# Attention with sinks and expert routing in one kernel: banded heads in 64-key blocks, routing steps in other places, sink values loaded by DMA

## The chip, the cores and the metric

One core of a Trainium2 chip runs one program. The metric is the device time in microseconds (us). Five engines work side by side, each through its own list of instructions in order: PE (matrix products, with PEld for its weight loads), DVE and ACT (both read PE's accumulators, PSUM), POOL (casts, memsets, and the issue of software DMAs), and SP (issue of the other DMAs). All DMAs run on the same 16 DMA engines. Instructions wait for each other through semaphores. The order within each engine is the order of the program text: the kernel uses a manual schedule.

## The reference

There are two parts, and the second reads what the first wrote.

```
attention, B=4, H=8, S=768, D=64, scale 1/sqrt(D):
    scores = scale * q @ k^T, causal
    heads 0, 2, 6 ("retrieval"): all earlier keys
    heads 1, 3, 4, 5, 7 ("banded"): keys 0..3 (sinks) and the last 64 keys
    out = softmax(scores) @ v
x = out as 3072 tokens x 512
mixture of experts, E=8, F=1024:
    for each expert e: rows = tokens with domain_id == e
        out[rows] = relu(x[rows] @ w1[e]) @ w2[e]
```

q, k, v and the weights arrive as float32; the products are done in fp16 with float32 sums.

## The kernel before

**Attention.** Heads are taken in pairs, `PAIRS = [(0, 2), (6, 7), (1, 3), (4, 5)]`, four pairs to a batch and 16 pairs n in all (n = 4 * batch + pair). The first pair has two retrieval heads (called RR here), the second one of each kind (RS), the third and fourth two banded heads (SS). The two heads of a pair lie on the two halves of the 128 partitions, so score products contract over 64 rows and come as two row tiles.

For each pair: `load_qk` and `load_v` (SP, lines 148 and 167) bring q, k and v four pairs ahead; `cast_qk` (line 158, POOL, two pairs ahead) and `cast_v` (line 178, POOL, one pair ahead) make fp16. `cast_v` also copies the four sink rows of each banded head into the small tiles `vs` (line 182), whose other rows are zero. PE transposes q and k of the next pair (line 286) into buffers of the pool `ps_b` (two buffers of one PSUM bank); DVE copies them out (line 292) as `qT`, `kT`.

`scores` works in rounds: a round is a score tile of 1024 columns (two banks) in the pool `ps_s` (three buffers). First PE adds masks by a product with the identity (line 306, `c16s`), then the products of `kT` and `qT` (also line 306); ACT takes the exponential of the whole tile (line 343) into `eT`. RR pairs have 6 rounds, RS pairs 5, SS pairs 3. A banded head is cut in key blocks of 128, each with the 192 query columns that see it, and extra columns "s" for the sinks.

The values are multiplied in by `av_items` (line 396): `eT` is the stationary operand and v with a column of ones the moving one (65 columns), summed in a `ps_b` buffer for each head; DVE takes reciprocals (line 408) and scales into `xb` (line 409). In the loop over n, pair n's score rounds go two at a time, and between them stand the transposes of pair n + 1 and the value products of pair n - 1:

```python
        elif R == 3:
            steps = [T["q"] + A, T["k"] + B_]
        ...
        for x, step in enumerate(steps):
            if n < NPAIR:
                scores(n, range(2 * x, min(2 * x + 2, R)))
            if n >= 1 and route:
                route.pop(0)()
            run(step)
```

**Routing.** `routing_items` computes from `domain_id` where each token goes: 20 small steps, nearly all on DVE, from `one_hot` (line 466) to `rows3` (line 637). One step is taken from the list in each step of the loop, from pair 1 on. Two of the steps have products on PE (`ranks`, line 484, and `rows`, line 595), both in `ps_b` buffers.

**The seam.** The finished heads of a batch, `xb`, are stored to DRAM (`store_x`, line 420, SP). `hooks(n)`, called ahead of pair n, holds the loads, the casts, the stores (batches 0, 1, 2 at n = 5, 9, 13), and weight loads by software DMA on POOL (line 190): w1 of expert 0 at n = 6, of experts 1 and 2 at n = 12 and 13. At n = 14 POOL clears four tiles (line 825), gathers the rows of experts 0 to 3 from the first three batches by six indirect DMAs (line 663), then issues w1 of expert 3, two more gathers and w2 of expert 0 (line 197). After the last pair PE transposes the first gathered rows (`x_transpose`, line 683, DVE copies in lines 690 and 696), then does the value products of pair 15; the store of batch 3 and the gathers that need all four batches follow.

**Experts.** `layer1` (line 711 on PE, 718 on ACT) takes 256 early slots of experts 0 to 3 first, then the rest; `layer2` (lines 761, 745) and `layer2_half` (line 775) give rows that DVE copies (line 725) into `oute` tiles of the pool `opool` and POOL scatters (line 727). A fallback for uneven routing (line 932) is not taken.

The softmax here doesn't subtract the row's maximum and nothing guards it: scores larger than these inputs give would overflow.

## Time and profile before

| what | value |
|---|---|
| median of 4 runs | 214.42 us (213.64 to 216.2) |
| profiled execution | 216.23 us, span 214.5 us |
| PE busy | 188.9 us (88%) |
| PEld, DVE, ACT, POOL busy | 123.4, 96.5, 92.3, 120.5 us |
| exponentials L343, 68 of them | 57.6 us |
| score products L306 (276) and masks L306 (132) | 24.9 and 22.7 us |
| value products L396 with ve (472) | 25.5 us |
| software DMA queue q0, hardware queue q1 | 55.1% and 36.9% of 16 engines |
| HBM read and written | 56.76 and 10.49 MB |

The span runs from the first to the last instruction on the chip; the rest of the time lies around it. A row with L306 names the line of the kernel that issued it, then engine and operation, what is written and read, the count, the busy time and the mean. PE's instructions overlap, so a mean of 200 ns does not say that one starts every 200 ns. The DMA row counts how busy the 16 DMA engines were, slice by slice.

### The profile page before, as it was taken

The page shows a single profiled execution, that of the slowest core. Times are in us where ns is not written, and L with a number is a line of the kernel's source. Part 1 is how long each engine was busy: PE and PEld are TensorE (multiplying, and loading weights), DVE is VectorE, ACT ScalarE, POOL GpSimd, SP SyncE. Part 2 cuts the span into 40 slices and gives each one's busy share as a digit, 9 for nine tenths or more (in the row PEclk, how much of TensorE's full clock was granted, in tenths as well). Part 3 has the DMA queues.
Part 4 walks back from the last instruction along what each step waited for, and adds up shares of the span by engine and source line. Part 5 has one row for each costly group of instructions (what it writes and reads, how often), then busy time and mean ns, then how long its engine had stood idle before and what let it go on. Part 6 is the DMA issues. An engine that isn't in the chain of part 4 may idle for free. (4 is left out here: it accounts for less than half of the span.)

```text
span 214.5 us, 4791 instructions
## 1 busy us (share of the span) xinstructions
PE 188.9 (88%) x1959; PEld 123.4 (58%) x1959; DVE 96.5 (45%) x200; ACT 92.3 (43%) x120; POOL 120.5 (56%) x170
## 2 busy tenths in 40 slices
PE   1699888999989999969859999999999999999950
PEld 1447555666656757649748996555655565444430
DVE  1345998899887657651110212540044400333420
ACT  2567545874786688614615562005610065100000
POOL 2417765697467697277645653557847720304772
PEclk9999996999999999979988999999999999999995
DMA  6999999999999999738999999999799999961443
GB/s 199 323 289 308 287 280 310 305 343 247 284 303 343 269 207 240 170 103 223 210 239 210 213 260 219 244 187 265 150 192 220 274 212 220 286 170 50 173 152 105
DMA packets 42909, 49.79 MB, mean 232 GB/s; under 512 B 27263, under 2 KB 35712, under 8 KB 42882
## 3 DMA queue, kind: packets, MB, share of 16 engines
q0 software_dynamic: 7936, 26.75, 55.1%
q1 hardware_dynamic: 34802, 22.62, 36.9%
q8 instruction: 17, 0.28, 0.5%
q10 hardware_dynamic: 144, 0.07, 0.2%
q14 instruction: 10, 0.08, 0.1%
HBM read 56.76 MB, written 10.49 MB: 314 GB/s over the span
## 5 line engine op out<-in xcount | busy, mean ns | idle before, releaser
L343 ACT ACTIVATE eT<-sp 128x1024 f16<-128x1024 f32 (+2 forms) x68 | 57.6, 918 | 27.7 <-PE sp L306 27.7
L718 ACT ACTIVATE hT<-h 128x512 f16<-128x512 f32 (+2 forms) x48 | 32.1, 669 | 59.1 <-PE h L711 59.1
L711 PE MATMUL h<-xT,w 128*128 128x256 f16 (+2 forms) x384 | 52.9, 300 | 0.5 <-DVE xT L690 0.5
L727 POOL DMA_INDIRECT out_dram<-oute,out_i x27 | 27.1, 1002 | 38.0 <-DVE oute L725 33.5
L711 PEld LDWEIGHTS <-w 128*128 128x128 f16 x384 | 39.8, 116 | 12.1 <-DVE xT L690 0.7
L761 PE MATMUL o<-w,hT 128*128 128x512 f16 x184 | 41.9, 379 | 0.0
L725 DVE COPY oute<-o 128x512 f32<-128x512 f32 x23 | 15.9, 692 | 51.5 <-PE o L761 50.0
L663 POOL DMA_INDIRECT xe<-x_tok,map_i x24 | 24.4, 1019 | 16.4 <-issue 6.3
L761 PEld LDWEIGHTS <-hT 128*128 128x128 f16 x184 | 17.5, 98 | 19.8 <-issue 0.8
L396 PE MATMUL av<-ve,eT 128*128 128x65 f16 (+1 forms) x472 | 25.5, 200 | 1.5 <-DVE xb L409 1.1
L306 PE MATMUL sp<-qT,kT 64*128 64x192 f16 (+8 forms) x276 | 24.9, 285 | 1.8 <-DVE kT L292 1.8
L396 PEld LDWEIGHTS <-eT 128*128 128x128 f16 (+1 forms) x572 | 22.7, 104 | 6.1 <-DVE xb L409 3.0
L306 PE MATMUL sp<-c16s 128*128 128x128 f16 (+1 forms) x132 | 22.7, 283 | 1.6 <-ACT eT L343 1.4
L158 POOL CAST q<-q 128x768 f16<-128x768 f32 x15 | 12.4, 829 | 15.8 <-DMA q<-in_q_dram 11.1
L696 DVE COPY xT<-xtp 128x1024 f16<-128x1024 f16 (+1 forms) x16 | 8.8, 552 | 27.1 <-PE xtp L683 27.1
L292 DVE COPY qT<-tpq 128x768 f16<-128x768 f16 x15 | 14.3, 953 | 12.2 <-PE tpq L286 12.2
L178 POOL CAST ve<-v 128x384 f16<-128x384 f32 x32 | 16.8, 553 | 5.1 <-DMA v<-in_v_dram 4.9
L409 DVE TENSOR_TENSOR xb<-av,rcp 128x384 f16<-128x384 f32 x32 | 17.8, 557 | 1.1
L158 POOL CAST k<-k 128x768 f16<-128x768 f32 x15 | 13.4, 896 | 8.4 <-PE tpk L286 6.6
L306 PEld LDWEIGHTS <-kT 64*128 64x128 f16 (+1 forms) x276 | 11.1, 98 | 12.2 <-issue 3.9
L292 DVE COPY kT<-tpk 128x768 f16<-128x768 f16 x16 | 15.3, 954 | 3.6 <-PE tpk L286 3.5
L286 PE MATMUL tpq<-c16s,q 128*128 128x128 f16 x96 | 9.4, 242 | 5.6 <-DVE q L158 4.8
(83 smaller groups left out, 136.9 us busy)
## 6 DMA issues: line engine op xcount, KB each, us to landing
w<-in_moe_w_dram POOLq DMA_DIRECT2D x16, 1024.0 KB, 12.4
q<-in_q_dram SPq DMA_DIRECT2D x16, 384.0 KB, 6.0
k<-in_k_dram SPq DMA_DIRECT2D x16, 384.0 KB, 5.9
v<-in_v_dram SPq DMA_DIRECT2D x32, 192.0 KB, 5.6
x_tok<-xb SPq DMA_DIRECT2D x4, 768.0 KB, 6.5
out_dram<-oute,out_i POOLq DMA_INDIRECT x27, 6.7
xe<-x_tok,map_i POOLq DMA_INDIRECT x24, 7.1
c16s<-c SPq DMA_DIRECT2D x1, 336.5 KB, 5.6
```

Source lines behind the costliest of these rows:

```text
L158: eng.tensor_copy(out=t[:].rearrange("p t h d -> p h t d"), in_=q32_t[nm, n][:])
L178: nc.gpsimd.tensor_copy(out=ve_t[b][:, :, h, 0:D], in_=v_t[b, pi][:, hh])
L292: evac(out=d[:], in_=cell["ps"][:, 0:NSO].rearrange("d t p -> d p t"))
L306: nc.tensor.matmul(out=sp[rows, c : c + w], lhsT=lhsT, rhs=rhs, start=bank not in begun, stop=True, skip_group_check=True,)
L343: nc.scalar.activation(out=eT[n, r // 3][:, r % 3, c0:c1], in_=sp[:, c0:c1], func=AF.Exp, scale=scale)
L396: nc.tensor.matmul(out=ps[m0:m1, it, :], lhsT=eT[n, r // 3][:, r % 3, c : c + w], rhs=rhs, start=(x == 0), stop=(x == len(mms) - 1), skip_ ...
L409: nc.vector.tensor_tensor(out=xb[b][:, :, h * D : (h + 1) * D], in0=ps[:, :, 0:D], in1=rcp[:].unsqueeze(2).to_broadcast([P, NSO, D]), op=A ...
L663: nc.gpsimd.indirect_dma_start(out=xe_of(pr, g), out_offset=None, in_=x_d[0 : 1 + nb * S, :], in_offset=bass.IndirectOffsetOnAxis(ap=map_i ...
L711: nc.tensor.matmul(out=pv[:, a, c0:c1], lhsT=w_t[e, 1][:, c // 2, c % 2, fc * 512 + fr : (fc + 1) * 512 : 4], rhs=xT_t[e][:, c, c0:c1], st ...
L718: nc.scalar.activation(out=hT_t[e][:, 2 * f2 : 2 * f2 + 2, c0:c1], in_=pv[:, :, c0:c1], func=AF.Relu)
L727: inst = nc.gpsimd.indirect_dma_start(out=out, out_offset=bass.IndirectOffsetOnAxis(ap=out_i[:, s : s + 1], axis=0), in_=o[:], in_offset=None,
L761: nc.tensor.matmul(out=ps[:], lhsT=hT_t[e][:, f, g * P : (g + 1) * P], rhs=w_t[e, 2][:, f // 4, f % 4, :], start=(f == 0), stop=(f == 7),)
```

## The change

It has four parts.

1. **Banded heads in 64-key blocks.** The key blocks of a banded head are now 64 keys with 128 query columns each; two blocks (even and odd) stand above each other in the 128 partitions, so a band needs 768 columns. Each product is a 64x64 tile of the array (64 rows, 64 columns of weights). The sinks are 32-key products of 256 query columns, each group of queries r on partitions 32r to 32r + 31. RS pairs have 4 rounds instead of 5, SS pairs 2 instead of 3. The value products of a banded head are 6 full ones (diagonal block 0 and the sinks), 5 over the lower 64 rows and 10 over the upper 64 rows with 64 columns.
2. **Transposes.** q and k are transposed together. In pairs with two rounds they go into one `ps_s` buffer ahead of the scores, and ACT copies q; elsewhere they go to the two `ps_b` buffers after the first two rounds, and DVE copies both.
3. **Routing.** A table places each step: one_hot to place in pair 0, place2 to high in pair 1, the rest at pairs 4, 5, 8, 10, 11, 12. A step now follows the products of its loop step. `rows` sums in a `ps_s` buffer.
4. **Sinks.** The `vs` tiles hold the sinks of 15 heads (two batches), one tile for each 32-partition place, in buffers of `opool`. Three are cleared on POOL and loaded by software DMA at the start, three are cleared on DVE at n = 1 and loaded at n = 4. The 20 small copies in `cast_v` go.

```diff
-    VS = [[7, 1, 4], [3, 5]]
+    VH, VR = 15, 3
...
+    m_even = neg(np.where(up, cc < kk, cc >= kk))
+    m_odd = neg(np.where(up, cc >= kk, cc < kk))
+    m_first = neg((ii[:, :P] >= jj) & ((jj < NS) | (ii[:, :P] - jj < WIN)))
...
-        for hh, h in enumerate((hA, hB)):
-            if not retr[h]:
-                x = 1 if hh and not retr[hA] else 0
-                nc.gpsimd.tensor_copy(
-                    out=vs_t[b % 2][x][64 * x : 64 * x + NS, VS[x].index(h), :],
-                    in_=ve_t[b][0:NS, 0, h, :],
-                )
+    def vs_tile(r, bh, eng):
+        t = opool.tile([P, 1024], FP16, tag="oute", name=f"vs_{r}_{bh}")
+        eng.memset(t[:], 0.0)
+        vs_t[r, bh] = t[:, 0 : VH * (D + 1)].rearrange("p (h d) -> p h d", h=VH)
+        eng.memset(vs_t[r, bh][32 * r : 32 * r + NS, :, D : D + 1], 1.0)
+
+    def load_vs(r, bh):
+        nc.gpsimd.dma_start(
+            out=vs_t[r, bh][32 * r : 32 * r + NS, :, 0:D],
+            in_=v.rearrange("b h j d -> j (b h) d")[
+                0:NS, 2 * H * (bh + 1) - VH : 2 * H * (bh + 1), :
+            ],
+        )
...
+    def s_bin(col, hh, part):
+        res = []
+        q0, q1 = ((0, 512), (512, S))[part]
+
+        def add(k0, m, o, i0, w, kind="band"):
+            lo, hi = max(i0, q0), min(i0 + w, q1)
+            if lo < hi:
+                res.append((col + lo - q0, hi - lo, hh, k0, m, o, lo, (hh, kind)))
+
+        for o in (0, 64):
+            add(o, 64, o, 0, P)
+        for it in range(NSO):
+            k0 = it * P
+            if it:
+                add(k0, 64, 0, k0, P)
+            add(k0 + 64, 64, 64, k0 + (64 if it else P), P if it else 64)
+        if part == 1:
+            for r in range(4):
+                i0 = (P, 3 * P, 4 * P, 4 * P)[r]
+                res.append((col + 256, 256, hh, 0, 32, 32 * r, i0, (hh, "s", r)))
+        return res
...
+    def transposes(n, q_evac, wide):
+        if wide:
+            ps = ps_s.tile([P, 2, 8, P], FP16, tag="sp", name=f"tp_{n}")
+            halves = [ps[:, x] for x in range(2)]
+        else:
+            halves = [
+                ps_b.tile([P, 8, P], FP16, tag="b", name=f"tp{nm}_{n}")[:] for nm in "qk"
+            ]
...
+                nc.tensor.matmul(
+                    out=sp[o : o + m, c : c + w],
+                    lhsT=kT[n][rows, k0 : k0 + m],
+                    rhs=qT[n][rows, i0 : i0 + w],
+                    start=False,
...
+                full.append((slice(0, P), band(0), ve[:, 0, h, :], 0, 0, P))
+                for it in range(1, NSO):
+                    r = (it - 1) // 2
+                    full.append(
+                        (slice(0, P), col_of(tiles, (hh, "s", r), it * P),
+                         vs_t[r, b // 2][:, b % 2 * H + h - 1, :], it, 0, P)
+                    )
+                for it in range(1, NSO):
+                    low.append((slice(0, 64), band(it * P), ve[0:64, it, h, :], it, 0, P))
+                    for m0 in (64, 0):
+                        jt = it if m0 else it - 1
+                        upp.append(
+                            (slice(64, P), band(it * P + m0), ve[64:P, jt, h, :], it, m0, 64)
+                        )
...
+        return (fa + fb, la + lb + ua + ub) if lb else (fa, fb)
...
-            t_ = ps_b.tile([P, 512], FP32, tag="b", name="map_ps")
+            t_ = ps_s.tile([P, 1024], FP32, tag="sp", name="map_ps")
...
+        return {
+            (0, 0): (one_hot,), (0, 1): (ranks, scan), (0, 2): (own, place),
+            (1, 0): (place2, split), (1, 1): (flags, high),
+            (4, 0): (high2, high3), (4, 1): lows[0:1], (4, 2): lows[1:2], (5, 1): lows[2:3],
+            (8, 0): lows[3:4], (8, 1): lows[4:5], (8, 2): lows[5:6],
+            (10, 0): (rows,), (11, 0): (rows2,), (12, 0): (rows3,),
+        }
...
-    for i in range(2):
-        for x in range(2):
-            nc.gpsimd.memset(vs_t[i][x][:], 0.0)
+    for r in range(VR):
+        vs_tile(r, 0, nc.gpsimd)
+        load_vs(r, 0)
...
+        if n == 1:
+            for r in range(VR):
+                vs_tile(r, 1, nc.vector)
+        if n == 4:
+            for r in range(VR):
+                load_vs(r, 1)
...
+        R = len(plans[n % 4]) // 2 if n < NPAIR else 1
+        av0, av1 = av_items(n - 1) if n >= 1 else ([], [])
+        tr = []
         if n == NPAIR:
-            steps = [[lambda: x_transpose(0, 0, 1, wide=True)] + A + B_]
...
+            tr = [lambda: x_transpose(0, 0, 1, wide=True)]
+        elif n + 1 < NPAIR:
+            q_evac = nc.scalar.copy if R == 1 else nc.vector.tensor_copy
+            tr = [lambda: transposes(n + 1, q_evac, R == 1)]
+        if R == 1:
+            run(tr)
+        steps = {1: [av0 + av1], 2: [tr, av0 + av1], 3: [tr, av0, av1]}[R]
         for x, step in enumerate(steps):
             if n < NPAIR:
-                scores(n, range(2 * x, min(2 * x + 2, R)))
-            if n >= 1 and route:
-                route.pop(0)()
+                scores(n, (2 * x, 2 * x + 1))
             run(step)
+            for fn in route.get((n, x), ()):
+                fn()
```

## The prediction

> **What bounds the kernel now.** I read the page's slices first, then the table of busy time by stretch, then the timelines of DVE, POOL and PE around the seam between attention and experts; landings of single DMAs, packets and clock stretches are from the trace's own records. The weight loads in their order are called w0, w1, w2, w3 (first-layer weights of experts 0 to 3). First the DMA row of the 40 slices, then the table by stretch:
>
> ```profile
> DMA  6999999999999999738999999999799999961443
> ```
> ```profile
> 60.00:75.00 15.00, 14.55 (x244) 10.08 (x243) 11.29 (x25) 10.14 (x13) 9.57 (x20) 1.00 1.06 301
> 75.00:90.00 15.00, 14.46 (x236) 9.70 (x233) 9.71 (x19) 11.70 (x15) 9.82 (x17) 1.00 1.03 219
> 90.00:98.00 8.00, 6.07 (x77) 4.61 (x76) 3.67 (x9) 1.95 (x4) 6.18 (x7) 0.79 0.36 93
> 98.00:115.00 17.00, 13.59 (x121) 12.33 (x120) 2.07 (x3) 7.09 (x13) 9.70 (x10) 0.90 1.03 232
> ```
> The columns are stretch, length, busy time of PE, PEld, DVE, ACT and POOL, clock, DMA share, GB/s. The DMA engines are full from 2 to 90 us (slices at 9), then at 0.36 for 8 us, then full again. So attention may compute faster, but its bytes and the first three expert weights end near 91.4 whatever the engines do. What can be won is that hole: 8.0 x (1 - 0.36) = 5.1 us of DMA time.
>
> The timelines of DVE, of POOL and of PE at that seam (start, length, and in brackets the idle time before and what ended it):
>
> ```profile
> 78.49 0.56 DVE L409 TENSOR_TENSOR xb<-av,rcp 128x384 f16<-128x384 f32 x1
> ```
> ```profile
> 78.88 0.70 POOL L190 DMA_DIRECT2D w<-in_moe_w_dram  x1
> ...
> 81.11 3.63 POOL L825 MEMSET xe<- 128x1024 f16 x4
> 89.27 1.09 POOL L663 DMA_INDIRECT xe<-x_tok,map_i  x1 [4.53 <-DVE xb L409]
> ```
> ```profile
> 92.38 0.38 PE L683 MATMUL xtp<-c16s,xe 128*128 128x128 f16 x4 [1.09 <-DMA xe<-x_tok,map_i]
> 93.60 0.40 PE L683 MATMUL xtp<-c16s,xe 128*128 128x128 f16 x4 [0.84 <-DMA xe<-x_tok,map_i]
> ...
> 109.83 0.63 PE L683 MATMUL xtp<-c16s,xe 128*128 128x128 f16 x8 [3.42 <-DMA xe<-x_tok,map_i]
> ```
> Why the hole is there: the normalised heads of pair 11 are ready at 79.05, SP then stores batch 2 (issued 79.07, landed 88.4), and only then do the six first gathers leave POOL, one each 1.3 us (1.0 busy, 0.3 issue). The fourth expert's weights (w3) stand behind them on POOL, at 96.9, and land at 109.3; the gathers behind w3 land after it, at 109.7. That is PE's gap of 3.42 us before 109.83. From 118.3 PE has no gap that matters (34.5 busy of 35 us from 115 to 150). The end is thus set by when the store of batch 2 is issued, not by the end of attention: PE waits at 91.3 already.
>
> **The change, part by part.** Durations are of the profiled execution: 216.23 us, span 214.5 and 1.7 around it. It lies 1.8 above the median of 214.42; PE had a half-clock stretch at 32.7 to 36.1 in it.
>
> *Pairs of two banded heads (SS), PE.* PE's timeline in pair 11, the later of them without routing:
> ```profile
> 68.94 1.04 PE L306 MATMUL sp<-c16s 128*128 128x512 f16 x4
> 69.91 0.62 PE L306 MATMUL sp<-qT,kT 64*128 64x192 f16 x12
> 70.45 0.51 PE L286 MATMUL tpq<-c16s,q 128*128 128x128 f16 x6
> ...
> 71.21 0.34 PE L396 MATMUL av<-ve,eT 128*64 128x65 f16 x5
> 71.48 0.23 PE L306 MATMUL sp<-c16s 128*128 128x64 f16 x2
> ```
> Pair 11 takes 4.46 us. Starts in the trace: masks 216 ns apart, then 312 to the first score; transposes 56 apart; value products (AV) 29.5 apart, whether 128 or 64 columns of weights; at 71.2 and 71.5 a change between 128-column and 64-column tiles shows as 122 to 129. So a change of tile shape costs 312 - 216 = 96 ns. Before there are nine such changes in an SS pair; after, six (masks, 64x64 scores, 64x32 sinks, full AV, lower halves, upper halves, transposes).
> New SS pair: 12 transposes x 56 = 0.67; masks 2 x 216 + 2 x 108 = 0.65; 28 scores in 64x64 tiles: 768 columns to a tile, at 53 ns per 128 (the score pairs of now) 0.32 if four tiles overlap, 28 x 29 = 0.81 if weight loads pace them: 0.60, towards the second, as the 64-column AV row paces at 29 to 36. 8 sink products of 256 columns: 0.11 all at once, 0.43 by twos: 0.25. AV 12 full x 29.5 = 0.35, 30 halves x 29.5 = 0.88 (0.60 if twos overlap). Switches 6 x 96 = 0.58. Sum 3.98, ends 3.3 and 4.4, against 4.46 where no routing disturbs.
> The Trainium skill (TensorEngine Tiling (Array Packing), sections Key Properties and Restrictions) speaks against this part: a change of tiling mode drains the array, and column tiling switches fast weight load off. Row: 96 ns a drain, fewer drains than before, and PEld rows of 64*64 last 104 ns like those of 128*128 (105). By the row 3.98; by the rule taken hard, weight loads that nothing hides, 36 score products x 104 ns = 3.7 us replace 0.85 and the pair takes 6.8. I keep the row: now the 64-column products start 29 to 36 ns apart, so their loads are hidden.
>
> *Transposes* go to a score buffer in SS pairs, with the query copy on ACT: 7 x 0.80 = 5.6 us onto ACT, 7 x 0.95 = 6.7 off DVE. The stall for a ps_b buffer (0.22 in pair 11) goes. Exponentials: 56 instead of 68 per kernel. Per batch 5 x 1.02 + 0.40 (two retrieval heads, RR), 3 x 1.02 + 0.70 (mixed, RS), 4 x 1.02 (two SS) = 13.3, 53.3 instead of 57.6. With the copies ACT stays at 59: no gain, but SS needs 2.85 of 4 us, so it is not the bound there. RR 4.9 and RS 4.8 (now 4.75 and 5.06 without routing) are near ACT's 9.3 for both.
>
> *Routing from pair 0.* On DVE the steps one_hot to high, about 9.5 us, fall into pairs 0 and 1, with three new memsets of about 0.6 each (0.27 for the 256-wide one, doubled). After kT of pair 1 (near 12.4) DVE has some 14.5 us queued, so the q and k copies of pair 2, the normalising of pair 0 and the k copy of pair 3 run late, to about 28. PE also waits in pair 0 for rs before the prior product, about 1.2. Pair 2 starts near 22 (21.17 now), and pairs 2 and 3 win nothing though they shed their routing (now 5.5 and 5.0): pair 4 at about 32 (31.68 now). The product of rows moves to a score buffer: nothing.
>
> *Sinks first.* POOL runs 3 x (0.95 + 0.1 + 1.0) = 6.2 us from 0.75, to 6.9 with the ve memset. Now it idles until 6.70 for v, and the next cast waits for q until 8.84: hidden; uncovered 0.2. The 20 copies of L182 (5.4 us) go; three issues (3 us) come in pair 4, ahead of casts whose data is 5 us early. c16 shrinks by 112 KB, the sinks read 92 KB: DMA unchanged.
>
> *Sum to the store.* Pairs 4 and 5 stay on DVE (high2, high3, three lows 3.9 us, copies and normalising 6.8: 10.7); 6, 7 8.1; 8, 9 9.8; 10, 11 8.1; 1.7 for keys of pair 10 delayed, as w0 is now issued earlier; pair 12 4.9: 32 + 10.7 + 8.1 + 9.8 + 8.1 + 1.7 + 4.9 = 75.3, normalised by 76 instead of 79.05. SP can then issue at 76: its last load was issued at 73.6. The store queues behind v of pair 15 (landed 77.4) and shares with w1. From first packet to landing it took about 6.4 us beside the weights (82.0 to 88.4): lands at 83.8. By the skill (DMA: Bandwidth & Descriptors, section Queues, rings and completion order: rings take turns packet by packet) its own 3.2 us (store 1, after v's landing) would double at most to 6.4 if packets were equal; same size, so the row stands. POOL is past its memsets at 83.3 in any case. w1 and w2 cannot come earlier: they stand on POOL behind casts of q and k of pairs 14 and 15, which land at 72.5 and 76.
>
> *Sum to the end.* Gathers leave at 84 to 92; they sit behind w2 in POOL's DMA queue, so the first lands at 91.8 to 92.3, as now, but the second with it: -1.0. w3 is issued at 92.8 instead of 96.9; the hole closes; w3 lands near 102.8 and the next gathers at 103.5, before PE wants them (105.4): -3.4. The half clock at 111.2 to 114.6, which follows that gap: -1.7; a copy wait at 118.3: -0.5. PE alone: -6.6. But the late gathers of expert pair 1 land at 122.4 and PE takes them at 122.74 now: they come earlier only by the filled hole, 5.1. So -5.2: **211.0 us**. The median does not move this: DMA's floor is the same in a run without the early half clock, so against 214.42 it is 3.4 less.
>
> **Rivals.**
> *The store comes no earlier* (0.20). SS pairs 6, 7, 10, 11 at 4.8 instead of 4.03, or DVE's queue, give 76 + 3 = 79. For: DVE is 95% busy in pairs 2 and 3; the new 64x64 pace is shown by no row. Against: six switches for nine. Then 214.4, within 1.5.
> *Tiles do not overlap* (0.16, slower). Place: 64x64 scores and 64x32 sinks. Price: 3072 + 2048 columns one after another at 53 ns per 128 = 2.1 instead of 0.85: SS 5.3. It decides from 4.8 on. The store is issued at 76 + 4 x 1.27 + about 1.5 (pairs 2, 3, RS) = 82.6, 3.5 later than now; all behind it moves: 214.4 + 3.5 = 218. For: the rules above. Against: pairs of row tiles start 3 to 4 ns apart, and so do 64-column pairs of L775.
> *The gathers need not wait for w2* (0.06). Then PE transposes at 87.5 and the end moves 5 more: 206. Against: every gather issued behind a weight load lands after it (7.1 us median, 2.8 at least).
>
> **Numbers.** Forecast (0.58): 211.0, own range 208.5 to 213.5. Less than 1% from 214.42, about what a measurement tells from nothing, is 212.3 to 216.6. Faster: 0.55 of the forecast, 0.06, 0.03 of the first rival: 0.64. Slower: 0.16 and a little of the first: 0.17. Same 0.19. Range 208 to 216: the forecast's own, the first rival, and the nearer part of the slower one. That the change would not do what it says is no rival: the instruction lists of the two programs show the tiles, the moved steps and the early loads.
>
> **What the changed profile would show.** Right: DMA share near 1 from 90 to 98; first gather issued near 84; store of batch 2 near 76; SS pairs near 4.0 late, pair 4 at 32; no half clock near 111; POOL's start hidden. Wrong if: SS over 4.8, or the first gather not before 88 (no gain), or PE waits at xtp L683 after 105 as long as now.

## The result: slower by about 1%, and the profile after

| | kernel before | changed kernel |
|---|---|---|
| median, all executions | 214.35 us (63: 211.55 to 217.45) | 217.01 us (42: 213.52 to 221.66) |
| ratio, 95% interval | 1 | 1.0074 (1.0049 to 1.0099) |
| profiled execution: time, span, mean clock | 216.23, 214.5 us, 0.966 | 218.41, 216.6 us, 0.956 |
| exponentials, score products, masks | 57.6 (68), 24.9 (276), 22.7 us (132) | 50.1 (56), 21.9 (468), 17.4 us (112) |
| expert pair 0 starts layer 2 (first product o2_0_0) | 129.79 us | 130.79 us |

The ratio compares, for each kernel, only the executions within 1.5% of its fastest; between the medians of all executions it is 1.012. The forecast was 211.0 us, 1.6% faster.

The DMA row of the 40 slices, then the table by stretch (length, busy PE, PEld, DVE, ACT, POOL, clock, DMA share, GB/s), of the changed kernel:

```profile
DMA  6999999999999999859999999996799999941333
```
```profile
75.00:90.00 15.00, 10.54 (x263) 7.79 (x263) 8.08 (x18) 8.34 (x9) 10.66 (x15) 0.95 1.07 233
90.00:98.00 8.00, 5.51 (x63) 4.51 (x64) 2.10 (x5) 0.57 (x1) 6.23 (x7) 0.50 0.53 119
98.00:115.00 17.00, 16.28 (x161) 15.47 (x160) 2.99 (x6) 9.08 (x17) 7.36 (x9) 0.98 0.98 222
115.00:150.00 35.00, 31.70 (x256) 22.15 (x254) 8.85 (x18) 10.16 (x19) 20.32 (x22) 0.95 1.01 227
```
PE has less to do in 75 to 90 (10.5 us busy instead of 14.5) and works at half clock from 90 to 98. From 98 to 115 it is busy 2.7 us more than before; from 115 to 150 it is busy 2.8 us less than before. So it wins the old gap and loses another. The hole in the DMA row has only gone from a share of 0.36 to 0.53.

The timeline of POOL at the seam (start, length, and in brackets idle time before and what ended it); the weight loads in it are w2, w3, and the second-layer weights of expert 0:

```profile
79.47 0.71 POOL L193 DMA_DIRECT2D w<-in_moe_w_dram  x1
...
87.49 1.10 POOL L649 DMA_INDIRECT xe<-x_tok,map_i  x1 [2.78 <-DVE rcp L395]
...
95.15 0.79 POOL L193 DMA_DIRECT2D w<-in_moe_w_dram  x1
...
98.59 0.78 POOL L200 DMA_DIRECT2D w<-in_moe_w_dram  x1
107.47 1.04 POOL L649 DMA_INDIRECT xe<-x_tok,map_i  x1 [8.11 <-SPq L924]
```
and PE's transposes in its timeline:
```profile
92.49 1.01 PE L669 MATMUL xtp<-c16s,xe 128*128 128x128 f16 x8 [6.15 <-DMA xe<-x_tok,map_i]
...
107.03 0.61 PE L669 MATMUL xtp<-c16s,xe 128*128 128x128 f16 x8 [0.21 <-DMA xe<-x_tok,map_i]
...
120.32 0.40 PE L669 MATMUL xtp<-c16s,xe 128*128 128x128 f16 x4 [1.93 <-DMA xe<-x_tok,map_i]
122.08 0.40 PE L669 MATMUL xtp<-c16s,xeh 128*128 128x128 f16 x4 [1.36 <-DMA xeh<-x_tok,map_i]
```
In the kernel before, POOL's timeline had at the place of its row at 107.47:

```profile
101.63 1.05 POOL L663 DMA_INDIRECT xe<-x_tok,map_i  x1 [0.49 <-issue]
```
The old gap of 3.42 us before the gather (1,3) is 0.21. The new one is at 107.47 on POOL: it waits 8.1 us for the store of batch 3 ("store 3" from here, as "store 2" for batch 2), so the gathers that need all batches, and the weights behind them, leave 5.8 us later than before (107.47 against 101.63), and PE waits for two of them at 120.3 and 122.1. After that wait stands a half-clock window (granted clock 0.5), 122.6 to 126.0. Store 3 was issued at the same time in both kernels (96.71, 96.78), but landed at 100.86 before and at 106.70 now. What differs is w3: 0.2 us behind the store before, 1.6 us ahead of it now.

That is what the change did to the order. w3 follows the first gathers, which follow store 2, which comes earlier now. Store 3 follows the value products of pair 15, which stand on PE behind the transposes xtp_0_0, and these wait for w2 to land (91.39 before, 91.97 now). So one side of the pair moved up and the other did not.

The new pair of two banded heads (SS), on PE's timeline in pair 11:

```profile
66.07 0.81 PE L312 MATMUL sp<-c16s 128*128 128x512 f16 x4
66.81 0.78 PE L329 MATMUL sp<-qT,kT 64*64 64x128 f16 x36
67.52 0.20 PE L383 MATMUL av<-ve,eT 128*128 128x65 f16 x1
...
67.99 0.91 PE L383 MATMUL av<-ve,eT 64*128 64x65 f16 x30
68.83 0.29 PE L312 MATMUL sp<-c16s 128*128 128x128 f16 x2
```
36 score products in 0.71 us: the tiles overlap. The step is 2.76 us; this one holds no transposes (those of pair 12 are done ahead of it). With transposes, in pair 6, it is 3.59 in the second trace of the changed kernel, without waits; in this first trace it was 4.69 in pair 6 and 5.40 in pair 10, with waits.

### The profile page after: what moved, and what is told of

It is laid out like the page before. It is cut to its first block, busy times and chain, and to the rows that moved or that the text cites. A ratio compares the mean times of both kernels' runs of the same rounds, so it can differ in the third digit from the quotient of the medians.

```text
span 216.6 us, 5346 instructions
## 1 busy us (share of the span) xinstructions
PE 182.8 (84%) x2231; PEld 122.7 (57%) x2231; DVE 94.5 (44%) x199; ACT 90.4 (42%) x115; POOL 121.7 (56%) x158
## 4 chain that ended last, share of the span: by engine, by line
issue 17%; PE 12%; DMA 10%; POOL 8%; POOLq 2%; DVE 1%; DVEq 0%
DMA w<-in_moe_w_dram 5%; PE o L747 5%; DMA xeh<-x_tok,map_i 4%; PE h L697 4%; POOL out_dram L713 4%; POOL xe L649 3%; PE o2h L761 2%; DMA out_dram<-oute,out_i 1%; PE xtp L669 1%; POOLq L1015 1%; POOL xeh L649 1%; POOLq L906 1%; POOL w L193 1%; DVE oute L711 0%; PE o_last L731 0%
## 5 line engine op out<-in xcount | busy, mean ns | idle before, releaser
L340 ACT ACTIVATE eT<-sp 128x1024 f16<-128x1024 f32 (+2 forms) x56 | 50.1, 953 | 15.6 <-PE sp L329 15.3
L697 PEld LDWEIGHTS <-w 128*128 128x128 f16 x384 | 40.7, 117 | 11.6 <-DVE xT L676 0.6
L383 PEld LDWEIGHTS <-eT 128*128 128x128 f16 (+2 forms) x672 | 21.3, 102 | 6.0 <-issue 3.3
L383 PE MATMUL av<-ve,eT 128*128 128x65 f16 (+2 forms) x572 | 22.8, 196 | 1.4 <-DVE kT L302 0.7
L329 PE MATMUL sp<-qT,kT 64*64 64x128 f16 (+8 forms) x468 | 21.9, 258 | 1.4 <-issue 0.8
L312 PE MATMUL sp<-c16s 128*128 128x128 f16 (+2 forms) x112 | 17.4, 275 | 0.7 <-ACT eT L340 0.5
L329 PEld LDWEIGHTS <-kT 64*64 64x64 f16 (+2 forms) x468 | 10.3, 104 | 9.6 <-issue 5.1
L669 PE MATMUL xtp<-c16s,xe 128*128 128x128 f16 x96 | 8.4, 226 | 8.3 <-DMA xe<-x_tok,map_i 8.3
L669 PEld LDWEIGHTS <-xe 128*128 128x128 f16 x96 | 6.7, 102 | 11.2 <-issue 7.5
L293 PEld LDWEIGHTS <-q 128*128 128x128 f16 x96 | 6.2, 105 | 9.8 <-DVE q L154 4.9
```

Source lines behind the costliest of these rows:

```text
L312: nc.tensor.matmul(out=sp[:, c : c + w], lhsT=id_sb, rhs=c16[:, col : col + w], start=c // 512 not in begun, stop=True, skip_group_check=True,
L329: nc.tensor.matmul(out=sp[o : o + m, c : c + w], lhsT=kT[n][rows, k0 : k0 + m], rhs=qT[n][rows, i0 : i0 + w], start=False, stop=True, skip ...
L340: nc.scalar.activation(out=eT[n, r // 3][:, r % 3, c0:c1], in_=sp[:, c0:c1], func=AF.Exp, scale=scale)
L383: nc.tensor.matmul(out=ps[m0 : m0 + m, it, :], lhsT=eT[n, r // 3][rows, r % 3, c : c + m], rhs=rhs, start=(cell["n"] == 1), stop=(cell["n" ...
L669: nc.tensor.transpose(out=ps[:, x, c, :], in_=xe_of(pr, g)[:, c1 * 256 + r : (c1 + 1) * 256 : 2], identity=id_sb,)
L697: nc.tensor.matmul(out=pv[:, a, c0:c1], lhsT=w_t[e, 1][:, c // 2, c % 2, fc * 512 + fr : (fc + 1) * 512 : 4], rhs=xT_t[e][:, c, c0:c1], st ...
```

## The experiments

Gathers and transposes are named by expert pair and group: (1,3) is group 3 of experts 2 and 3, xtp_1_3 its transposes. Theory A: the order of store 3 and w3 cost the gain. Theory B: the DMA engines are full from 98 us on, so only bytes put in the hole count. Theory C: the tail is POOL's, by its drain and the scatters behind it. Theory D: attention and the start of the experts are bound by loads, so PE's saving is hidden. Ratios are to the kernel before, with 95% intervals.

### Does store 3 suffer by standing behind w3?

First, w3 moved behind two gathers in the changed kernel, twice:

```diff
-            load_w(3, 1)
             for g in (3, 4):
                 load_xe(1, g, 3)
+            load_w(3, 1)
             load_w(0, 2)
```


> The changed kernel with the weight load w3 (expert 3, first layer) issued behind the two gathers (1,3) and (1,4) instead of ahead of them; nothing else moves. Two gathers take 2.6 us of POOL, so w3 leaves at about 97.8 us instead of 95.15, that is behind the store of batch 3 (96.8), as it did in the kernel before. Theory A (w3 ahead of the store is what cost the gain): the store lands at 100 to 102 us instead of 106.70, the late gather (0,2) leaves at 101 to 103 instead of 107.47, the second-layer weights of expert 1 leave by 107 instead of 111.13, the PE waits of 2.2 and 1.6 us before the transposes xtp_1_2 and xtp_1_6 go, and with them the half-clock window at 122.7 to 126.1; o2_0_0 starts 3 to 5 us earlier (126 to 128 instead of 130.79) and the time falls to 212 to 215. Theory B (the DMA engines are full from 98 us on and only bytes put in the hole before it count): the store lands earlier but everything behind it lands as late as now, the stall moves to w3 (layer 1 of expert 3), o2_0_0 stays within 1 us of 130.8 and the time within 1 us of 217.

> The changed kernel with w3 behind the gathers (1,3) and (1,4) once more, with more rounds, since its four runs (215.99, ratio 1.0015 to 1.0206) could not be told from the changed kernel's. Theory A alone: o2_0_0 at 126 to 128.5 again instead of 128.5 to 130.8, a ratio of 0.995 to 1.004, that is 1 to 2.5 us less than the changed kernel. If the order of w3 and the store is not worth anything in the time, the ratio stays at 1.007 to 1.012.

Measured: store 3 landed at 101.17 and 100.90, the late gather (0,2) left at 101.94 and 101.67, the waits before xtp_1_2 and xtp_1_6 went (but for 1.0 us before xtp_1_2 in the first run; 1.1 and 1.2 us came before xtp_0_6), o2_0_0 began at 127.14 and 127.54. POOL's timeline in the second of them:

```profile
96.03 0.80 POOL L193 DMA_DIRECT2D w<-in_moe_w_dram  x1
...
101.67 1.07 POOL L649 DMA_INDIRECT xe<-x_tok,map_i  x1 [4.08 <-SPq L924]
```
In the trace theory A is right within a microsecond. In the time it is hardly there: 215.99 us, ratio 1.0111 (1.0015 to 1.0206), then 217.21, 1.0066 (1.0030 to 1.0102). In the second trace PE stood level with the kernel before at o2_0_0 (127.54; 127.77 in the second trace of that kernel) and lost the rest behind it, where the change touches nothing: 0.9 us in a wait behind POOL's drain (see the part on the tail), and the last scatter took 4.7 us to land instead of 2.6. Why the scatter did is open (see the last section).

Then the mirror, in the kernel before: store 3 held on its queue until ACT's first hidden tile is written.

```diff
+    layer1(0, 0, EARLY, (0, 1))
+    hold = rpool.tile([P, 8], FP16, name="hold")
+    nc.sync.dma_start(out=hold[:], in_=hT_t[0][:, 0, 0:8])
     store_x(B - 1)
...
-    layer1(0, 0, EARLY, (0, 1))
```


> The mirror of the run that moved w3: the kernel before, with the store of batch 3 held on its queue until ACT has written the first hidden tile of expert 0 (a 2 KB copy from that tile goes ahead of it), so that it leaves at about 98.8 instead of 96.71, two us behind w3 (96.92) as in the changed kernel; PE's work is the same. Theory A: the store now takes 9 to 10 us instead of 4.2 and lands at 107 to 109 instead of 100.86, the late gather (0,2) leaves at 108 to 110 instead of 101.63, the second-layer weights of expert 1 at 112 to 113 instead of 105.29, PE waits 1 to 4 us for (0,2) to (1,6), and the time grows by 1.5 to 4 us, to 215.5 to 218. If the order against w3 does not matter, the store lands 2 us later and the time stays within 1 us of 214.2.

```profile
96.45 0.78 POOL L190 DMA_DIRECT2D w<-in_moe_w_dram  x1
...
110.62 1.04 POOL L663 DMA_INDIRECT xe<-x_tok,map_i  x1 [9.96 <-SPq L934]
```
The store left at 98.27, 1.8 us behind w3, and landed at 109.84; PE waited at four late transposes (5.7 us), o2_0_0 came at 133.73. 218.69 us, ratio 1.0194 (1.0112 to 1.0276). A store that left 1.6 and 2.9 us later than in the two traces of the kernel before cost some 4 us of the time: theory A's mechanism is shown, here in the time too.

The kernel before, a second trace, and the changed kernel, again:

> The kernel before, unaltered, for a second trace. By theory A its store of batch 3 leaves within 0.5 us of w3 and takes 4 to 5 us (4.2 in the first trace); one half-clock window or none between 85 and 105; o2_0_0 at 127 to 129, since the execution of the first trace (129.79) was 1.9 us slower than the median. If o2_0_0 stands at 129.5 or later while the time is at the median, what the changed kernel loses lies behind it, in the tail.

> The changed kernel itself, unaltered, beside the others of this set, since its times spread over 8 us: it should stand at 1.005 to 1.012 of the kernel before. In its trace the two things that theory A names must be seen again if they are no accident of one execution: w3 issued one to two us ahead of the store of batch 3, and the store landing 9 to 10 us after its issue (106.70 - 96.78 in the first execution), against 4.2 us in the kernel before; and two to four half-clock windows of 3.4 us in a row from about 88 us on.

Before: 213.83 us, store 3 issued at 95.36, w3 at 95.40, landed at 99.36, one half-clock window at the seam, o2_0_0 at 127.77. So this execution, near the median, is 2 us better at o2_0_0 than the first trace (129.79). Changed: 217.99 us (22 executions), ratio 1.0095 (1.0053 to 1.0137); w3 0.5 us ahead of the store, which took 7.6 us; o2_0_0 at 128.51. So at o2_0_0 the changed kernel stood 1.0 us behind in the first two traces and 0.7 in the second two. In the second two PE came to the wait before xtp_0_0 at the same time (89.0), since attention had lost its lead (see the part on loads). All traces together, for store 3:

| kernel (traces) | issued against w3 | issue to landing |
|---|---|---|
| before (2), before with fewer loads; w3 moved (3) | 2.3 us ahead to 0.1 behind | 3.8 to 5.5 us |
| av 15 first, all versions (6) | 1.8 to 6.5 us ahead | 3.7 to 4.5 us |
| changed (2), no drain, PE kept busy, routing as before, fewer loads; w2 late (behind w2) | 0.5 to 4.5 us behind | 7.6 to 10.0 us |
| before, store held | 1.8 us behind | 11.6 us |

### The half clock

30 products that nobody reads, ahead of xtp_0_0; then 20 of them with w3 moved as above:

```diff
+            def warm():
+                ps = ps_s.tile([P, 1024], FP32, tag="sp", name="warm")
+                for i in range(30):
+                    nc.tensor.matmul(
+                        out=ps[:, 0:512], lhsT=id_sb, rhs=c16[:, C_S1 : C_S1 + 512], start=True, stop=True
+                    )
-            tr = [lambda: x_transpose(0, 0, 1, wide=True)]
+            tr = [warm, lambda: x_transpose(0, 0, 1, wide=True)]
```


> The changed kernel with 30 idle products (128x512, into a score buffer that nobody reads, nothing of the computation changed) on PE ahead of the transposes xtp_0_0, where PE waits from 85.0 to 92.5 for the first gathers; at 216 ns each they fill 6.5 us. If the half-clock windows from 88.5 to 98.8 are PE's own (it idled), they go: the av products of pair 15 and layer 1 of expert 0, which run at half speed from 92.5 to 98.8, come 2 to 3 us earlier, the store of batch 3 leaves at about 94.5, ahead of w3 (95.15), so lands by 99, and by theory A the late gathers follow as in the kernel before: o2_0_0 at 125 to 127.5, the time 212 to 214.5. If the late gathers are bound by the DMA engines (theory B), o2_0_0 stays at 129 or later and the time within 1 us of the changed kernel's. If the windows come for another reason, nothing moves.

> The changed kernel with w3 behind those two gathers and 20 idle products on PE (4.3 us at 216 ns) ahead of xtp_0_0: the two edits together, of which the second alone won nothing. If the half-clock windows cost time only where no later wait takes the gain back, they now count: layer 1 of expert 0 runs at full clock from about 94, the late gathers leave at 101 to 103, o2_0_0 at 123.5 to 125.5, ratio 0.985 to 0.995 (211 to 213). If the half clock is of no weight, the time is that of the move of w3 alone.

PE's and POOL's timelines of the first:

```profile
85.22 1.10 POOL L649 DMA_INDIRECT xe<-x_tok,map_i  x1 [0.18 <-POOL xe L817]
...
107.53 1.04 POOL L649 DMA_INDIRECT xe<-x_tok,map_i  x1 [10.17 <-SPq L930]
```
```profile
85.20 6.65 PE L841 MATMUL warm<-c16s 128*128 128x512 f16 x30
93.95 0.66 PE L669 MATMUL xtp<-c16s,xe 128*128 128x128 f16 x8 [2.11 <-DMA xe<-x_tok,map_i]
```
The half-clock windows at 88 to 98 come from PE's wait: with PE kept busy they went but for one at 95.3 to 98.7, and the mean clock (median of all executions) rose from 0.954 to 0.972, near that of the kernel before (0.974). The time did not move: 218.22, ratio 1.0103 (0.9999 to 1.0208), and o2_0_0 came at 130.59, where 125 to 127.5 was expected. Expected was that the store would leave ahead of w3; it did not. Here store 2 went ahead of w1 and landed at 81.1, so the gathers and w3 left 2 us earlier (w3 at 92.88), while store 3 left at 97.34 and landed at 106.76. The half clock alone costs nothing that this interval shows, while a later wait takes its place. With w3 moved as well the ratio is 1.0032 (0.9989 to 1.0075), 217.34 us: on the way of theory A, but its interval overlaps the others, and o2_0_0 was 128.72 in its trace, against 123.5 to 125.5 expected, with a new wait of 1.75 us for w3 itself.

### The value products of pair 15 ahead of the wait

```diff
-        if R == 1:
+        if R == 1 and n < NPAIR:
             run(tr)
-        steps = {1: [av0 + av1], 2: [tr, av0 + av1], 3: [tr, av0, av1]}[R]
+        steps = {1: [av0 + av1 + (tr if n == NPAIR else [])], 2: [tr, av0 + av1], 3: [tr, av0, av1]}[R]
```


> The changed kernel with the order on PE changed in the last step alone: the av products of pair 15 come ahead of the transposes xtp_0_0 instead of behind them, so that they run while PE waits for the first gathers (85 to 92.5 us), and batch 3 is stored from about 90 instead of 96.8. Theory A (the store of batch 3 standing behind w3 cost the gain): the store lands by 95, the late gathers (0,2), (0,6), (0,5) leave right behind w4 at about 99.5 instead of 107.47, layer 1 of expert 0 starts 2 to 3 us earlier, the stalls before xtp_1_2 and xtp_1_6 go, o2_0_0 starts at 123 to 127 and the time falls to 209 to 214. Theory B (DMA full from 98 on): late loads land when they did, PE waits for them elsewhere, o2_0_0 at 129 or later, 215 to 217. Theory C (the end is set by POOL's drain and the twelve scatters behind it, which wait for the last weight load): o2_0_0 comes earlier by what theory A says, but the end follows only as far as the last weight load (landed at 193.1) comes earlier.

> The changed kernel with the av products of pair 15 ahead of xtp_0_0 once more, with more rounds. If the changed kernel's loss is all in the seam (store of batch 3 behind w3, av 15 behind the wait for the gathers, the half clock), it stands level with the kernel before with the same move: ratio 0.986 to 0.995, o2_0_0 at 124 to 126.5. If part of the loss lies elsewhere (in attention, or in the tail) the ratio is 0.996 to 1.003.

PE's timeline in the first of them:

```profile
87.53 1.10 PE L383 MATMUL av<-ve,eT 64*128 64x65 f16 x30
91.86 1.01 PE L669 MATMUL xtp<-c16s,xe 128*128 128x128 f16 x8 [3.24 <-DMA xe<-x_tok,map_i]
```
Store 3 left at 89.90 and landed at 93.90; o2_0_0 at 125.15. 212.62 us, ratio 0.9898 (0.9791 to 1.0004), then, over 22 executions, 212.53, 0.9932 (0.9899 to 0.9964), as expected; its o2_0_0 was not (127.70 in an execution of 215.34 us, where 124 to 126.5 was expected). One edit takes the whole loss away. Is it a merit of the change? The kernel before with the same move:

> The kernel before with the same move as the run that gave 212.6: the av products of pair 15 ahead of the transposes xtp_0_0. It tells what of the gain of that run belongs to the change of the heads. In the kernel before, PE works until about 88.5 and waits to 92.4, the store of batch 3 left at 96.71 and was hardly held up (4.2 us), and the wait for the gather (1,3), behind w3, cost 3.4 us before 109.83. With av 15 first the store leaves at 91 to 93 and the late gathers up to 3 us earlier, but (1,3) stays behind w3, which stays behind the first gathers (issued at 96.9), so that wait stays: 0 to 1.5 us won, 212.5 to 214.5. If it wins as much as the changed kernel did from the move (4 us, 210 to 211), the banded columns themselves bring nothing once the seam is in order.

212.80 us, ratio 0.9916 (0.9883 to 0.9949), o2_0_0 at 126.09. The two kernels stand level with it. So the order at the seam can make up the changed kernel's loss, as theory A says. It is not shown that all of the loss arises there: with the move the changed kernel keeps a wait behind POOL's drain (1.4 and 1.1 us, none in the kernel before; see the part on the tail). And its faster attention is worth nothing that these intervals show.

### Versions meant to beat both

The av products first, 15 idle products behind them, and the gathers (1,2), (1,6), (1,5) ahead of the second-layer weights of expert 1, in either kernel:

```diff
-    load_w(1, 2)
     for g in (2, 6, 5):
         load_xe(1, g)
+    load_w(1, 2)
```


> A version meant to beat both: the changed kernel with the av products of pair 15 ahead of xtp_0_0 (which alone gave 212.6), 15 idle products behind them (3.2 us at 216 ns, the wait from 88.6 to 91.9) to keep the clock, and the gathers (1,2), (1,6), (1,5) issued ahead of the second-layer weights of expert 1 instead of behind them. In the run with av 15 first the half-clock windows lasted until 98.4, 6.5 us of them while PE worked, so 3 us could be won; the gather (1,2) landed at 117.71 behind those weights, just as PE wanted it, so without the third edit the gain would be lost in that wait; ahead of them it should land by 112. By theory A (order of the loads, then the clock): o2_0_0 at 121 to 123.5 instead of 125.15, time 209 to 211.5. By theory B (DMA engines full): PE waits for w3 or the gathers instead and it stays at 212 to 213.5.

> The kernel before with the three edits of the version that took 211.2: the av products of pair 15 ahead of xtp_0_0, 15 idle products behind them, and the gathers (1,2), (1,6), (1,5) ahead of the second-layer weights of expert 1. It tells what the banded columns are worth once the seam is in order. If the first gathers are bound by loads (theory D: attention's own loads and w0 to w2 fill the DMA engines up to about 92 us, so that xtp_0_0 starts at 91 to 94 however soon attention is done), this kernel comes within 1 us of it: 210.5 to 212.5, xtp_0_0 at 91 to 93. If PE's shorter attention is worth what it saves (its pair 15 ended 3 us earlier), this kernel is 2 to 4 us slower: 213 to 215.

211.22 us, ratio 0.9880 (0.9808 to 0.9953), o2_0_0 at 123.03; and from the kernel before 211.96, 0.9867 (0.9795 to 0.9939), o2_0_0 at 123.17. Both beat the kernel before by the same 1.2 to 1.3%, and the changed kernel by more. xtp_0_0 began at 93.75 and 93.88 though pair 15 began 4.1 us earlier in the first (81.21 against 85.32). The o2_0_0 of 121 to 123.5 expected for the first holds for both; the idle products outlasted the wait in both (15 took 5.1 us in the first, at half clock, and 3.4 in the second, not 3.2).

Then w2 behind the first gathers alone (w1 and w3 stay where they are in the changed kernel), and a second version, in which w1 comes one pair later too, so that store 2 has nothing ahead of it. The second also has the av products first and the three gathers ahead, as above, without idle products. Its edit of the loads:

```diff
-        ws = {6: (0, 1), 12: (1, 1), 13: (2, 1)}
+        ws = {6: (0, 1), 13: (1, 1)}
...
                 load_xe(pr, g, 3)
-            load_w(3, 1)
+            load_w(2, 1)
             for g in (3, 4):
                 load_xe(1, g, 3)
+            load_w(3, 1)
```


> The changed kernel with the weight load w2 (expert 2, first layer) moved from pair 13 to behind the six first gathers, ahead of w3. The first gathers no longer stand behind it in the software queue, and the store of batch 2 has one load less beside it. If the gathers wait for w2 alone, the store of batch 2 lands at 84 to 86 (86.59), the first gather lands within 3 us of its issue, xtp_0_0 starts at 88 to 90 instead of 92.49 and the PE idle time and its half-clock windows shrink; w2 is issued at about 94, lands at 99 to 102, just ahead of its use at about 104, but w3 and all behind it land about 4 us later, since 1 MB is moved out of the stretch before 92. So by theory A the start gains 3 us and the late gathers lose it again: 215 to 218. By theory B (bytes in the hole are what counts) it loses 1 to 4 us: 218 to 221.

> A version meant to beat both: the changed kernel with the av products of pair 15 ahead of xtp_0_0, w1 one pair later (pair 13), so that the store of batch 2 goes ahead of it, w2 behind the six first gathers, then (1,3), (1,4), w3, and the gathers (1,2), (1,6), (1,5) ahead of the second-layer weights of expert 1. Where the store once happened to go ahead of w1 (75.65 against 76.48) it landed at 81.1 instead of 86.6, but the gather that left at 85.22 landed at 93.82, 0.36 us behind w2. With w2 behind the gathers it should land by 89, so xtp_0_0 starts at 88 to 90 instead of 92, with hardly a half-clock window; w2 lands at 98 to 100, w3 at 103 to 105, about as PE wants them: o2_0_0 at 119.5 to 122, time 207.5 to 210. If w2 or w3 come late (theory B, the bytes moved out of the stretch before 92 are missing later), PE waits 2 to 5 us there and the time is 211 to 214.

w2 alone: 219.52 us, ratio 1.0167 (1.0062 to 1.0272); xtp_0_0 began at 91.51, PE then waited to 111.9 for (1,3). As theory B had it. The second version: store 2 landed at 81.08, 5.1 us after its issue, the first gather at 89.16, xtp_0_0 at 89.30, all as forecast; then w3 was 1.0 us late and (0,2) and (0,6), behind w3 and the second-layer weights, 2.3 and 0.5 us. o2_0_0 came at 127.51 (119.5 to 122 expected). 215.93 us, ratio 1.0007 (0.9972 to 1.0041), 3.2 us earlier at the start and the gain of it gone by 113. Bytes moved out of the stretch before 92 were missed later.

### Is attention bound by its loads?

Loads of q and k from pair 3 on, and of v from batch 1 on, left out in both kernels (the tiles of the first pairs are used again):

> The changed kernel without the loads of q and k from pair 3 on and of v from batch 1 on: the first three pairs' q and k and batch 0's v are used again in their places (so the later heads are computed on wrong data). It measures attention without its loads. Theory D (attention of the changed kernel is bound by its loads): the pairs run at PE's or POOL's pace, banded pairs 2.8 to 2.9 us, mixed 5.2 to 5.6, the other 4.7 to 5.1, a batch in 15.5 to 16.5 us, so pair 15 starts at 75 to 78 instead of 82.5 and the store of batch 2 is out by 70. If PE bound it already, pair 15 starts within 1 us of 82.5.

> The kernel before without the same loads (later heads on wrong data in the same way). By theory D the kernel before was nearly bound by PE: banded pairs 4.4 to 4.5 us, a batch in 18 to 19, pair 15 starting at 83.5 to 87 instead of 87.66, so 7 to 10 us behind the changed kernel without the loads: that is what the banded columns save on PE. If loads bound it as much, it starts pair 15 before 82.

Table by stretch, 20 to 40 and 40 to 60 us, first the changed kernel without the loads, then with them; the last two columns are DMA share and GB/s:

```profile
20.00:40.00 20.00, 19.56 (x365) 14.01 (x364) 17.87 (x43) 13.56 (x16) 14.40 (x23) 1.00 0.05 8
40.00:60.00 20.00, 19.56 (x424) 14.50 (x422) 17.36 (x32) 16.43 (x20) 14.39 (x23) 1.00 0.49 130
```
```profile
20.00:40.00 20.00, 17.70 (x373) 12.65 (x372) 18.92 (x43) 14.57 (x17) 15.20 (x24) 1.00 1.13 292
40.00:60.00 20.00, 17.87 (x403) 13.07 (x399) 14.99 (x29) 14.98 (x18) 10.15 (x16) 1.00 1.09 286
```
Without loads PE is busy 98% and a batch (pair 4 to 8, 8 to 12) takes 16.9 and 17.4 us, against 19.7 and 19.4 with them; the kernel before takes 20.0 and 20.7 without, 21.4 and 20.4 with. So the change saves PE 3.2 us a batch, and loads take back 2 to 3 of it; the kernel before gains at most 1.4. They can take back all: in the second trace of the changed kernel pair 9 took 10.4 us instead of 6.2 (PE waited 2.1 us for the cast of k of pair 10, which had landed 13.1 us after its issue, beside w0, and then ran at half clock from 57.4 to 64.2; here that did cost time), and the two batches took 40.3 us together, against 40.0 in the second trace of the kernel before. Pair 9 was as long (9.9 and 10.5) in two other traces, with the same half clock. Theory D is right in direction; 15.5 to 16.5 was too good. The start of pair 15 says nothing (87.16 in the first, forecast 75 to 78), since pairs 12 and 13 took 8.6 and 9.2 us through another stall:

```profile
71.94 3.63 POOL L824 MEMSET xe<- 128x1024 f16 x4
72.07 3.54 DVE L617 TENSOR_SCALAR mb<-mu 128x28 int32<-128x28 int32 x1
```
An operation of DVE on 28 columns lasted 3.54 us beside four memsets of POOL; in the kernel before it lasts 0.16. PE waited for the copies of q and k around it, 2.5 us, and ran at half clock for 13.7 us. The whole execution took 216.52 us, so the time gained nothing from PE's saving.

### The tail, and a part undone

```diff
-            if (pr, g) == (2, 1):
-                nc.gpsimd.drain()
```


> The changed kernel without the drain on POOL that stands behind the scatter of expert 4's second group (it lasted 9.96 us, to 197.11, and 8.39 us, to 194.53, in the kernel before). Theory C (the tail is POOL's): scatters leave as their tiles are ready, from 188 on; the PE wait of 1.2 us before o2h_3 goes, the last scatter leaves about 0.8 us behind PE's last product instead of 2.5, and the time falls by 2 to 3.5 us, to 213.5 to 215. If the tail is PE's own, as the prediction took it, at most 0.5 us is won.

```profile
182.47 1.02 POOL L713 DMA_INDIRECT out_dram<-oute,out_i  x1 [11.38 <-DVE oute L711]
184.19 1.01 POOL L713 DMA_INDIRECT out_dram<-oute,out_i  x1 [0.70 <-DVE oute L711]
```
Scatters now leave one by one, PE's wait before o2h_3 (the half group of the last expert pair) is gone, and nothing is won: 217.96 us, ratio 1.0234 (1.0143 to 1.0325), rather slower than the changed kernel. The last drain of POOL took 6.55 us instead of 4.07; part of the cost only moved. Theory C falls as far as the middle drain should be worth 2 to 3.5 us. That the end hangs on POOL does not fall with it, for in the changed kernel with its drain PE's timeline has:

```profile
201.59 1.92 PE L761 MATMUL o2h<-w,hT 128*64 128x512 f16 x16 [1.17 <-DVE oute L711]
```
This wait is 1.2 and 1.4 us in the two traces of the changed kernel and none in the two of the kernel before. At PE's last product the changed kernel is 2.2 and 2.1 us behind (209.65 against 207.41, 207.54 against 205.46), at o2_0_0 only 1.0 and 0.7: more than half of the lag comes up behind the seam, in this wait. The drain ends 3.8 to 4.5 us after the last weight load lands in all 19 traces that have it, and in the changed kernel that load lands 2.3 and 1.8 us later. What holds it back is not shown.

Routing spread as before, one step a loop step from pair 1 on, in the changed kernel:

> A part of the change undone alone: the changed kernel with the routing steps spread as in the kernel before, one a step from pair 1 on. If the routing in pairs 0 and 1 is what makes pair 2 start late (23.3 us; 19.0 to 21.2 in the kernel before), it starts at 20 to 21.5, DVE having less in the first 20 us. By theory D (loads bound attention) pair 15 starts where it did (82 to 83.5) and the time stays at 216.5 to 218; if the late start is part of the loss, 214 to 216.

Pair 2 began at 24.75, not earlier; 217.43 us, ratio 1.0075 (1.0038 to 1.0111), the changed kernel's. The moved routing has no share that this interval shows, and pair 2's late start does not come from it (in this trace pair 1 still lasted 9.9 us).

## Why the prediction was wrong

- **SS pair.** Forecast 3.98 (3.3 to 4.4), measured 3.59 with transposes, against 4.46. Right in kind; the terms mis-sized are the scores (0.60 + 0.25 and two changes of shape: 1.04, measured 0.71) and the 20 upper value halves (0.59; measured 0.31: they start in pairs, 3 to 4 ns apart, with 26 to 50 ns from pair to pair). The row, not the hard reading of the rule on tiling, was right to be kept, and the rival in which tiles don't overlap is out: the result fell on its side for another reason.
- **Store 2 issued at 76:** 76.10, in part by luck: pair 4 began at 29.72 instead of 32, and pairs 4, 5 took 12.2 us instead of 10.7, pairs 8, 9 11.3 instead of 9.8. **Landing at 83.8:** 86.59. This was the first step to fail. I took 6.4 us beside the weights from the time of first packet to landing and let the store start at 77.4; issued 1.05 us behind w1, it took 10.5 us. Where it went 0.8 and 3.9 us ahead of w1 it took 5.5 and 5.1 (9.2 where it went only 0.2 ahead). The rule that I held beside the row there, that the queues take turns packet by packet (DMA: Bandwidth & Descriptors, in the Trainium skill, section Queues, rings and completion order), is not what decided: by it the order of issue would hardly matter, and the traces of store 3 show 3.7 to 5.5 us or 7.6 to 11.6 according to the order.
- **First gather lands with w2:** right (92.35, w2 at 91.97). Elsewhere a gather that left at 85.22 landed at 93.82, w2 at 93.46; one that left at 84.62 at 91.75, w2 at 91.40. **w3 at 92.8:** 95.15, so it filled less of the hole: 0.53 instead of near 1.
- **The gap before (1,3) and the half clock at 111:** right: -3.2 of the -3.4, and the window gone; PE was 4.5 us ahead at xtp_0_2 (112.71 against 117.20).
- **The late gathers earlier by the filled hole, 5.1:** this is the step that turned the sign. They landed at 120.27 and 122.03 instead of 121.69 and 122.38. I followed w3 past everything behind it on its own queue, and not past store 3 on SP's queue, which it now overtook. The -5.2 became +1.0 at o2_0_0.
- **Half clock:** charged for the old gap, not for the new one. PE's wait at the seam grew (6.15 us in one piece, and 6.2 us of the work behind it at half clock) because PE came to it 5.0 us earlier (86.34 against 91.29) and w2 did not. On its own it cost nothing that the run with PE kept busy shows.
- **"The end is set by when store 2 is issued":** no. Store 2 left 3.0 us earlier and landed 1.8 earlier; w2 landed when it did, and the first layer began when it did.
- **Nothing lost behind the seam:** the sum carried the -5.2 from the late gathers to the end unchanged. The wait before o2h_3 added 1.2 and 1.4 us there, which the prediction put at nothing.
- **ACT, start of POOL:** right in kind (ACT 90.4 busy in all instead of 92.3, the exponentials 50.1 where 53.3 was forecast; the cast of q that followed the sinks at 8.76 instead of 8.84).

Of the loss of 0.7 to 1.0%, what is shown: it is gone when av 15 goes ahead of the wait; a store behind w3 costs the time in the kernel before. Not shown is how much of the changed kernel's time is that pair alone: moving w3 mended the trace up to o2_0_0 and left a ratio of 1.0066 (1.0030 to 1.0102). The rest, the wait behind the drain among it, stays open.

## What to carry to other kernels

When a step comes earlier, look at what it overtakes on the other queues, not only at what follows it on its own: here a big load that moved from just behind a store to just ahead of it held that store about as long as the load lasted (9.9 and 11.2 us), and all that waited for the store with it. Work that is ready (here the value products, and the store behind them) belongs ahead of a wait for data on an engine that goes in order. And a faster engine in a stretch whose loads fill the DMA engines brought an earlier wait here, with a clock that fell in it; look for the edit that puts work into that wait first.

## What the runs showed of the hardware that I had not expected

- **Order between the two kinds of queue.** The 768 KB store of batch 3 took 3.7 to 5.5 us when issued ahead of a 1 MB weight load or level with it, and 7.6 to 11.6 when 0.5 to 4.5 us behind. In the first changed trace hardly a packet of it moved before 101, four us after its issue; from then on packets of both queues moved side by side. The same with loads in attention: q of pair 10 landed 11.9 us after its issue behind w0 (42.87 to 54.72, w0 at 42.56), and 5.6 before (w0 3.8 us behind it). Level with a load is no safe place: q of pair 11 in the kernel before, issued 0.1 us ahead of w0, took 11.5 us.
- **The software queue goes in order to the end:** the first gather, where w2 was issued ahead of it, landed 0.3 to 1.0 us behind w2 in all 12 traces that show both, whether it left 3 or 8 us before w2 landed. The first gather behind w3, where w3 was not moved, landed 0.3 to 1.0 us behind it in 14.
- **DVE beside POOL's memsets:** 0.16 us became 3.54, as shown above. The Trainium skill (SBUF — State Buffer, section SBUF: two separate sides) says that DVE and POOL share a pair of ports by a lock that one instruction holds to its end. The row agrees in kind, but the operation waited through four memsets in a row (3.63 us together; 0.95 or so would be one of them). That the lock is the reason is not shown.
- **The last scatter.** It landed 2.6 to 3.6 us after its issue in some executions and 4.2 to 4.9 in others, with nearly the same number of packets in the trace; in all, from its issue to the end of the span 4.1 to 5.0 us in 12 traces and 5.7 to 6.5 in 7 (without the middle drain 8.3). The three traces with w3 moved are all of the long kind, and so is the one with routing as before. No run tells why, and it weighs as much as the whole difference.
